# Splitting one routing into pieces on VectorE, and moving the low parts of w2 to GpSimd in whole tiles

## The chip, the cores and the metric

One Trainium2 chip, one of its cores. The metric is the device time of one launch in microseconds (us). TensorE (PE) does the matrix products, VectorE (DVE), ScalarE (ACT) and GpSimd (POOL) the elementwise work; SyncE (SP) and GpSimd issue the DMA transfers.

## What is computed

An mLSTM attention over 2 x 8 heads, 768 steps, head width 40; its output, as 1536 tokens of width 320, goes through a dense layer with softplus (320 to 2048 to 320), and the result through a mixture of 8 experts, in which each token takes the one expert with the largest logit. The part of the reference that the change lies in:

```python
def _moe2_ref(x, w_gate, w_output_gate, w1, w2):
    logits = x @ w_gate
    e_idx = np.argmax(logits, axis=1)
    ...                       # gate_w: the chosen expert's softmax weight; eom: a sigmoid gate
    for e in range(E):
        mask = e_idx == e
        h = np.maximum(x[mask] @ w1[e], 0.0)
        ye = h @ w2[e]
        out[mask] = gate_w[mask, None] * eom[mask, e, None] * ye
```

Everything is float32. The kernel forms the large products from operands split into a rounded high part and a low part (the rest), so that three products of the faster type (high x high, high x low, low x high) stand for one float32 product.

## The kernel before

**A planner orders the work.** The kernel is written as Python generators, the tasks. Each `yield "V"` (or "A", "G", "P", "S") is a request for a turn on VectorE (ScalarE, GpSimd, TensorE, SyncE); "VG" or "AV" leaves the planner the choice between two; `yield [events]` waits. `Weaver.run` (line 118) keeps a clock for each engine, made up of fixed costs, and gives the next turn to the task that can start first by these clocks, ties by rank. All instructions that a task issues between two yields go into the engine's queue in one piece. On the chip each engine then works through its queue in just that order and waits where an operand is not there, whether or not something behind it could run. A change of the yields so changes the order in the queues, and the planner's costs decide how.

**Dense layer and routing.** The 1536 tokens are cut into 6 blocks of 256 (`NBLK`, blk = 0 to 5). `up1` (line 1255) makes the products `ph` of a block with one of 16 column groups f, in PSUM banks of the ring `bank_h`; `softplus` (1227) does three ScalarE activations on `ab` (two buffers), then on VectorE `g` (which frees the `ab` buffer and the PSUM bank of `ph`), then the cast `gh` and the difference `gl`; `down1` (1278) adds the products of `gh` and `gl` with the second weight into `acc`. When a block's sum is near its end, `down1` starts `route(blk)` (915). It computes logits, counts tokens per expert with small products, and gives each token a row number (`posi`) in a table `rows` in DRAM that is sorted by expert in slots of 128 rows. Two `scatter` tasks (1207, indirect DMAs on GpSimd's queue) write the block's rows. The tail of `route` also carries the state (room left, next free slot) to the next block's routing, `state[blk + 1]`. This tail is 28 small VectorE instructions. Between its steps stands `yield from pause(blk)`, and `pause` (1051) yields in all blocks but blk = `NBLK - 2` = 4, the next to last. So the tail of block 4 is one piece in VectorE's queue, while the others can be interleaved with `g` and `gl`. Block 5 has a tail of its own, `place_last`.

**What waits for the scatters of block 4.** `early_rows` (1123) loads the first four slots (`er`) from `rows` once ten scatters, those of blocks 0 to 4, are done; `early_turn` (1152) transposes them on TensorE (`xe`) and adds the tokens of block 5 from the chip's own memory, so that the experts can begin before block 5 is in DRAM.

**Experts.** There are 15 slots (`NS`), each of one expert. The hidden width 1024 is done in 4 quarters of 256 columns (`NQ`, qn = 0 to 3). In each quarter `second` (1638) does, for pairs of slots, `up` (products `ph` with `w1s`, three PSUM banks), `halves_sum` (1581: a ScalarE copy `hr` and a VectorE sum `hr`), `turn_h` (1590: transposes `tp` into two PSUM banks) and `split_h` (1600: ScalarE `hh`, VectorE `hl`, which frees the bank of `tp`); then for all slots `down` (products `yp` with `w2s`) and `reduce2` (adds into `yac`). In the last quarter, `down` of the first slots is mixed in after slot 9, and each finished slot is written out by an indirect DMA from GpSimd.

**Weights.** For each quarter and expert, `w1raw` and `w2raw` come from DRAM into one ring of 7 buffers. `split_w2` (1422) casts the high part of a tile (128 x 640) on ScalarE, once the last `yp` of the quarter before has read the old `w2s`; `low_w2` (1448) subtracts it from the raw tile, which gives the low part, in two halves of 128 x 320: quarter 0 on GpSimd, the others "VG", on whichever of VectorE and GpSimd is free first by the planner's clocks. `w2_ready[qn]` needs all 8 experts before the first `yp` of the quarter. The raw buffer is free when both halves are done, and the next load in SyncE's queue waits for it: the load of expert 7 takes the buffer of expert 0. `low_w1` and `low_w1p` (1410, 1416) do the same for `w1`, at the end of a quarter.

Of the kernel before, what the change touches and what calls it, by code (L numbers as in the profile page):

```python
# [8 lines left out]
F32 = mybir.dt.float32  # L9
# [225 lines left out]
def mlstm_moe_kernel(ctx: ExitStack, tc: tile.TileContext, q_t, k_t, k, v, i_gate, f_gate, o_gate,  # L235
                     w_in, w_gate, w_og, w1, w2, out):
    nc = tc.nc
    W = Weaver()
# [8 lines left out]
    NQ, E, FQ = w1.shape[0], w1.shape[1], w1.shape[-1]  # L247
# [6 lines left out]
    NBLK = NCH  # L254
# [10 lines left out]
    G = B * H  # L265
# [524 lines left out]
    def psub(out_, a, b_):  # L790
        POOL.tensor_tensor(out=out_, in0=a, in1=b_, op=ALU.subtract)

    def vsub(out_, a, b_):
        DVE.tensor_tensor(out=out_, in0=a, in1=b_, op=ALU.subtract)
# [77 lines left out]
    def tt(out_, a, b_, op):  # L872
        DVE.tensor_tensor(out=out_, in0=a, in1=b_, op=op)
# [4 lines left out]
    def over(ap, n):  # L878
        return ap.unsqueeze(1).to_broadcast([ap.shape[0], n, ap.shape[1]])
# [35 lines left out]
    def route(blk, acc, full, part):  # L915
# [88 lines left out]
        yield "V"  # L1004
        tt(an, tot, room, ALU.is_gt)
        DVE.scalar_tensor_tensor(out=bn, in0=room, scalar=float(P), in1=tot, op0=ALU.add, op1=ALU.is_lt)
        yield from pause(blk)
        DVE.tensor_tensor_scan(out=cum, data0=newp, data1=more_p, initial=0.0, op0=ALU.add, op1=ALU.add)
        tt(m, rank, over(room, T2), ALU.is_ge)
        tt(nr, rank, over(nxt, T2), ALU.add)  # L1010
        yield from pause(blk)
        DVE.scalar_tensor_tensor(out=dn, in0=u, scalar=float(P), in1=base, op0=ALU.mult, op1=ALU.subtract)
        yield from pause(blk)
        tt(m, m, over(dn, T2), ALU.mult)
        DVE.tensor_scalar(out=ef, in0=ef, scalar1=1.0, scalar2=None, op0=ALU.add)
        yield from pause(blk)
        tt(nr, nr, m, ALU.add)
        DVE.scalar_tensor_tensor(out=ef, in0=ssum, scalar=1e-9, in1=ef, op0=ALU.add, op1=ALU.mult)
        yield from pause(blk)
        tt(nr, nr, ohb, ALU.mult)  # L1020
        DVE.reciprocal(out=row[:, :, CCOL], in_=ef)
        yield from pause(blk)
        DVE.tensor_reduce(out=pos, in_=nr, axis=AX.X, op=ALU.add)
        yield from pause(blk)
        DVE.tensor_copy(out=posi, in_=pos)
        placed = Event(W.cur.out)
        for t in range(T2):
            W.add(after(placed, after(whole[t], scatter(blk * TPB + t, row[:, t, :], posi[:, t:t + 1], row_ev))), 0)
        yield from pause(blk)
        tt(t8, an, dn, ALU.mult)  # L1030
        tt(c1, csi, rem.to_broadcast([P, E]), ALU.is_le)
        tt(room, room, tot, ALU.subtract)
        tt(c2, an, bn, ALU.add)
        yield from pause(blk)
        tt(nxt, nxt, t8, ALU.add)
        DVE.tensor_reduce(out=nmx[:, 0:1], in_=c1, axis=AX.X, op=ALU.add)
        tt(nmx[:, 1:2], total, rem, ALU.is_gt)
        DVE.scalar_tensor_tensor(out=room, in0=c2, scalar=float(P), in1=room, op0=ALU.mult, op1=ALU.add)
        DVE.scalar_tensor_tensor(out=s128, in0=total, scalar=float(P), in1=s128, op0=ALU.mult, op1=ALU.add)
        yield from pause(blk)  # L1040
        tt(nxt, nxt, tot, ALU.add)
        DVE.scalar_tensor_tensor(out=nmx[:, 1:2], in0=rem, scalar=0.0, in1=nmx[:, 1:2], op0=ALU.is_ge, op1=ALU.mult)
        W.signal(ev)
        yield from pause(blk)
        DVE.scalar_tensor_tensor(out=base, in0=room, scalar=s128, in1=nxt, op0=ALU.subtract, op1=ALU.add)
        DVE.scalar_tensor_tensor(out=esl, in0=nmx[:, 0:1], scalar=nmx[:, 1:2], in1=esl, op0=ALU.mult, op1=ALU.add)
        tt(rem, rem, total, ALU.subtract)
        W.signal(small_ev)
        W.signal(state[blk + 1])

    def pause(blk):
        if blk != NBLK - 2:
            yield "V"

    def place_last(small, tot, rank, ohb, ef, ssum, row, row_ev, ev, counts_ev, small_ev, blk, whole):
        T2, T8 = TPB, TPB * E
# [150 lines left out]
    def scatter(i, row, posi, row_ev):  # L1207
        yield "G"
        r = POOL.indirect_dma_start(
            out=rows, out_offset=bass.IndirectOffsetOnAxis(ap=posi, axis=0), in_=row, in_offset=None,  # L1210
            bounds_check=SLOTS * P - 1, oob_is_err=True)
        if i:
            tc.declare_no_dep(r.ins, group="scatter", reason="every token has a row of its own")
        tc.add_to_no_dep_group("scatter", r.ins)
        W.signal(row_ev)
        W.signal(scattered)
        if i < NTILE - TPB:
            W.signal(scattered_most)
# [55 lines left out]
    def after(t, gen):  # L1274
        yield [t if isinstance(t, Event) else Event(t)]
        yield from gen

    def down1():
        parts = {}
        yield [done_chunk[b][0] for b in range(B)]  # L1280
        for blk, f0, f1 in legs:
            acc, full = [], events(TPB)
            for t in range(TPB):
                acc.append((yield from bank_y.get([P, DM], F32, f"acc{t}")))
            if f1 < NF:
                if f0 == 0:
                    parts[blk] = (yield from row_ring.get([P, TPB, ROW], F32, "row", users=TPB)) + (None,)
                before, parts[blk] = parts[blk][2], parts[blk][0:2] + (events(TPB),)
            for f in range(f0, f1):
                yield [done_g[blk, f]]  # L1290
                gh, gl, e1, e2 = g_t.pop((blk, f))
                for t in range(TPB):
                    yield "P"
                    sl = slice(t * P, (t + 1) * P)
                    PE.matmul(acc[t][0], gh[:, sl], w_down(f, 0), start=f == f0, stop=False)
                    PE.matmul(acc[t][0], gh[:, sl], w_down(f, 1), start=False, stop=False)
                    PE.matmul(acc[t][0], gl[:, sl], w_down(f, 0), start=False, stop=f == f1 - 1)
                    if f == f1 - 1:
                        if f1 < NF:
                            W.add(after(W.cur.out, keep_part(*acc[t], parts[blk], t, before)), 1)  # L1300
                        else:
                            W.signal(full[t])
                W.signal(e1)
                W.signal(e2)
                W.signal(used_w[f])
                if f == NF - 2:
                    W.add(route(blk, acc, full, parts.get(blk)), 1)
# [14 lines left out]
    right = {}  # L1322
# [99 lines left out]
    def split_w2(qn):  # L1422
        if qn:
            yield [w2_read[qn - 1]]
        else:
            yield [down_done]
            right["w2s"] = big.tile([P, 2, 2, E, DM], F32R, tag="win", name="w2s")
        w2s = right["w2s"]
        for e in range(E):
            yield [w2_raw[qn, e]] + ([have_exps if e < E - 2 else begun[e - 4]] if qn == 0 else [])  # L1430
            r, ev = w2_t.pop((qn, e))
            yield "AV" if qn else "A"
            copy(w2s[:, 0, :, e, :], r)
            W.add(after(W.cur.out if qn else clear, low_w2(qn, e, r, ev)), 3.9)
# [11 lines left out]
        W.signal(clear)  # L1446

    def low_w2(qn, e, r, ev):
        for j in range(2):
            yield "VG" if qn else "G"  # L1450
            (psub if W.cur.on == "G" else vsub)(right["w2s"][:, 1, j, e], r[:, j], right["w2s"][:, 0, j, e].bitcast(F32))
        W.signal(ev)
        W.signal(w2_ready[qn])

# [71 lines left out]
    rp, w1s, w2s = right["pool"], right["w1s"], right["w2s"]  # L1526
# [291 lines left out]
```

## Time and profile before

| what | us |
|---|---|
| three runs: median (lowest to highest) | 429.84 (429.53 to 431.52) |
| the profiled execution: its own time | 428.57 |
| its span from first to last instruction | 426.9 |
| TensorE busy | 408.9 |
| VectorE busy | 341.4 |
| ScalarE busy | 302.1 |
| GpSimd busy | 186.0 |

The profile is one execution. Its granted TensorE clock was 0.996 of full speed over the span. The busy times say which engine has most to do on the whole; what a stage is worth has to be read in that stage, from the order of the instructions and from what each of them waited for.

### The profile page before, as it was taken

The numbers are of one execution on the slowest core, as the hardware profiler recorded it, in microseconds if no ns is written. First come the engines' busy times: TensorE is split into PE (matmuls) and PEld (weight loads), VectorE is DVE, ScalarE is ACT, GpSimd is POOL, SyncE is SP. The second block draws the span as 40 slices with busy tenths as digits, with TensorE's granted clock in tenths as the row PEclk, the third lists the DMA queues.
The fourth block names the chain that finished last, engine by engine and source line by source line (L and its number), as shares of the span: only waits on it lengthen the run. The fifth ranks groups of instructions, "written<-read, shape, count | busy, mean of one in ns | idle before, by whom it ended". The sixth has DMA issues, their size and how long they took to land.

```text
span 426.9 us, 9922 instructions
## 1 busy us (share of the span) xinstructions
PE 408.9 (96%) x3095; PEld 388.6 (91%) x3095; DVE 341.4 (80%) x914; ACT 302.1 (71%) x880; POOL 186.0 (44%) x272
## 2 busy tenths in 40 slices
PE   8899999999999999999999999989999999999994
PEld 7787999999989999999999999767998998898893
DVE  4998979889988999997765765767755898898863
ACT  3678889969767877876967887576798666565421
POOL 5265755665041102130210101237676487387665
PEclk9999999999999999999999999999999999999998
DMA  8959595571228981222100101318645745645022
GB/s 264 339 176 335 188 306 188 180 223 36 87 60 281 340 272 55 64 63 62 39 36 4 39 2 40 111 38 271 227 136 173 237 136 194 215 130 157 13 83 96
DMA packets 32284, 62.90 MB, mean 147 GB/s; under 512 B 4218, under 2 KB 16765, under 8 KB 32230
## 3 DMA queue, kind: packets, MB, share of 16 engines
q1 hardware_dynamic: 30742, 57.87, 43.1%
q0 software_dynamic: 1488, 4.35, 2.8%
q8 instruction: 28, 0.46, 0.5%
q14 instruction: 26, 0.21, 0.2%
HBM read 54.05 MB, written 8.65 MB: 147 GB/s over the span
## 4 chain that ended last, share of the span: by engine, by line
PE 71%; DMA 9%; DVE 7%; issue 4%; ACT 4%; POOL 3%; SPq 1%; POOLq 0%; ACTq 0%; DVEq 0%
PE ph L196 26%; PE acc L196 19%; PE yp L196 9%; PE pv L196 3%; PE sp L196 3%; DMA out_dram<-yac,tki 2%; PE tp L196 2%; DMA abc<-abc_dram 2%; DMA wra<-in_w_in_dram 2%; PE lg L196 2%; DMA vn<-in_v_dram 2%; POOL w2s L196 1%; DMA yac<-rows 1%; POOL out_dram L196 1%; SPq L196 1%
## 5 line engine op out<-in xcount | busy, mean ns | idle before, releaser
L196 ACT ACTIVATE ab<-ab 128x256 f32<-128x256 f32 x192 | 77.3, 415 | 2.6
L196 PE MATMUL ph<-w1s,flat 128*128 x312 | 60.7, 332 | 0.5 <-ACT flat L196 0.5
L196 POOL TENSOR_TENSOR w1s<-w1raw,w1s 64x256 fp32r<-64x256 f32 (+1 forms) x39 | 40.9, 1061 | 42.5 <-ACT w1s L196 22.0
L196 PE MATMUL acc<-win,gh 128*128 128x320 f32 x240 | 55.7, 317 | 0.0
L196 PE MATMUL yp<-w2s,hh 128*128 x240 | 54.6, 315 | 0.0
L196 DVE SCALAR_TENSOR_TENSOR g<-ph,ab 128x256 f32<-128x256 f32 x96 | 39.8, 419 | 15.9 <-ACT ab L196 15.0
L196 PEld LDWEIGHTS ph<-w1s,flat 128*128 128x128 f32 x312 | 46.7, 189 | 4.7 <-ACT flat L196 0.7
L196 ACT ACTIVATE ab<-ph 128x256 f32<-128x256 f32 x96 | 36.3, 378 | 17.5 <-PE ph L196 16.7
L196 DVE TENSOR_TENSOR gl<-g,gh 128x256 fp32r<-128x256 f32 x96 | 42.2, 445 | 7.7 <-ACT gh L196 6.7
L196 POOL TENSOR_TENSOR w2s<-w2raw,w2s 128x320 fp32r<-128x320 f32 x46 | 42.2, 952 | 8.9 <-ACT w2s L196 3.6
L196 POOL DMA_INDIRECT rows<-row,rsm x12 | 13.1, 1090 | 75.7 <-DVE nxt L196 29.7
L196 ACT CAST gh<-g 128x256 fp32r<-128x256 f32 x94 | 37.3, 398 | 11.1 <-DVE g L196 10.6
L196 ACT COPY hr<-ph 128x256 f32<-128x256 f32 x60 | 22.7, 378 | 29.5 <-PE ph L196 27.9
L196 PE MATMUL ph<-win 128*128 128x256 f32 x250 | 41.3, 286 | 0.6 <-DVE g L196 0.6
L196 PEld LDWEIGHTS yp<-w2s,hh 128*128 128x128 f32 x240 | 39.8, 188 | 1.5 <-issue 0.6
L196 DVE TENSOR_TENSOR hr<-ph,hr 128x256 f32<-128x256 f32 x60 | 24.7, 418 | 18.6 <-ACT hr L196 18.0
L196 PEld LDWEIGHTS acc<-win,gh 128*128 128x128 f32 x240 | 38.7, 189 | 0.5 <-ACT gh L196 0.2
L196 PE MATMUL acc<-win,gl 128*128 128x320 f32 x120 | 37.3, 311 | 0.0
L196 PE MATMUL yp<-w2s,hl 128*128 x120 | 37.2, 310 | 0.0
L196 PEld LDWEIGHTS ph<-win 128*128 128x128 f32 x250 | 34.4, 190 | 0.8 <-DVE g L196 0.8
L196 PE MATMUL acc<-wou,gh 128*128 128x320 f32 x144 | 33.3, 316 | 0.0
L196 ACT CAST w2s<-w2raw 128x640 fp32r<-128x640 f32 x32 | 22.8, 741 | 14.0 <-PE yp L196 14.0
(211 smaller groups left out, 1073.8 us busy)
## 6 DMA issues: line engine op xcount, KB each, us to landing
w1raw<-in_w_dram SPq DMA_DIRECT2D x32, 384.0 KB, 3.1
wra<-in_w_in_dram SPq DMA_DIRECT2D x16, 704.0 KB, 6.6
w2raw<-in_w_dram SPq DMA_DIRECT2D x32, 320.0 KB, 3.5
abc<-abc_dram SPq DMA_DIRECT2D x4, 1024.0 KB
rows<-pad SPq DMA_DIRECT2D x19, 194.0 KB, 6.0
qT<-in_q_t_dram SPq DMA_DIRECT2D x6, 512.0 KB, 4.6
kn<-in_k_dram SPq DMA_DIRECT2D x5, 416.0 KB, 7.5
vn<-in_v_dram SPq DMA_DIRECT2D x6, 320.0 KB, 5.7
```

Of the source, the lines that this page charges most:

```text
L196: return fn(*args, **kw)
```

## The change

Two edits. `pause` loses its argument and yields in every block, so the tail of the routing of block 4 is cut into twelve pieces, as in blocks 0 to 3. And `low_w2` makes the low part of a tile in one GpSimd instruction of 128 x 640 in quarters 0 to 2 and, in quarter 3, for six of the eight experts; experts 3 and 7 of quarter 3 are done in two halves on VectorE.

```diff
-        yield from pause(blk)
+        yield from pause()
         DVE.tensor_tensor_scan(out=cum, data0=newp, data1=more_p, initial=0.0, op0=ALU.add, op1=ALU.add)
...
-    def pause(blk):
-        if blk != NBLK - 2:
-            yield "V"
+    def pause():
+        yield "V"
...
     def low_w2(qn, e, r, ev):
-        for j in range(2):
-            yield "VG" if qn else "G"
-            (psub if W.cur.on == "G" else vsub)(right["w2s"][:, 1, j, e], r[:, j], right["w2s"][:, 0, j, e].bitcast(F32))
+        if qn < NQ - 1 or e % 4 != 3:
+            yield "G"
+            psub(right["w2s"][:, 1, :, e, :], r, right["w2s"][:, 0, :, e, :].bitcast(F32))
+        else:
+            for j in range(2):
+                yield "V"
+                vsub(right["w2s"][:, 1, j, e], r[:, j], right["w2s"][:, 0, j, e].bitcast(F32))
         W.signal(ev)
         W.signal(w2_ready[qn])
```

The first pair of lines stands for all eleven calls of `pause` in `route`, which change alike.

## Rows read from the trace of the kernel before

**Rows 1.** The page: shares of the span by engine in the chain that ended last.
```profile
PE 71%; DMA 9%; DVE 7%; issue 4%; ACT 4%; POOL 3%; SPq 1%; POOLq 0%; ACTq 0%; DVEq 0%
```
**Rows 2.** Timeline, routing of block 4 (start, us, engine, out<-in, count [idle before <-releaser]).
```profile
267.05 0.41 ACT L196 ACTIVATE ab<-ab 128x256 f32<-128x256 f32 x1
267.10 0.17 DVE L196 TENSOR_TENSOR newp<-lg,room 128x8 f32<-128x8 f32 x1 [0.86 <-ACT rsm L196]
268.65 0.17 DVE L196 CAST rsm<-rsm 128x2 uint32<-128x2 f32 x1
270.00 0.74 DVE L196 SCALAR_TENSOR_TENSOR g<-ph,ab 128x256 f32<-128x256 f32 x2
270.44 0.41 ACT L196 CAST gh<-g 128x256 fp32r<-128x256 f32 x1 [1.38 <-DVE g L196]
270.46 0.74 PE L196 MATMUL ph<-xh,wou 128*128 128x256 f32 x4 [0.81 <-DVE g L196]
```
**Rows 3.** Timeline: second scatter of block 4, load of the early rows, their first use.
```profile
270.98 1.17 POOL L196 DMA_INDIRECT rows<-row,rsm  x1 [0.30 <-ACT gh L196]
273.83 0.89 SPq L196 DMA_DIRECT2D er<-rows  x2
279.99 0.31 PE L196 MATMUL xe<-ident,er 128*128 128x128 f32 x1
```
**Rows 4.** Timeline of VectorE, routing of block 3: first step and row numbers.
```profile
251.46 0.17 DVE L196 TENSOR_TENSOR newp<-lg,room 128x8 f32<-128x8 f32 x1
254.38 0.16 DVE L196 CAST rsm<-rsm 128x2 uint32<-128x2 f32 x1
```
**Rows 5.** Waits from 300 us on (total us, times, longest us).
```profile
PE tp L196 <- DVE hl L196: 2.1, 3, 1.0
```
**Rows 6.** Timeline, start of quarter 2.
```profile
356.99 9.63 POOL L196 TENSOR_TENSOR w2s<-w2raw,w2s 128x320 fp32r<-128x320 f32 x10 [2.51 <-DVE yac L196]
358.15 0.33 SPq L196 DMA_DIRECT2D w2raw<-in_w_dram  x1
360.39 1.92 DVE L196 TENSOR_TENSOR w2s<-w2raw,w2s 128x320 fp32r<-128x320 f32 x2
360.95 0.69 ACT L196 ACTIVATE hh<-tp 128x256 fp32r<-128x256 f32 x2
362.57 0.74 DVE L196 SCALAR_TENSOR_TENSOR hl<-tp,hh 128x256 fp32r<-128x256 f32 x2
362.63 0.79 ACT L196 CAST w2s<-w2raw 128x640 fp32r<-128x640 f32 x1
363.03 0.77 PE L196 MATMUL tp<-ident,hr 128*128 128x128 f32 x4 [0.99 <-DVE hl L196]
```
**Rows 7.** Timeline, quarters 1 and 3: low parts on GpSimd, TensorE's wait, first product.
```profile
325.46 3.89 POOL L196 TENSOR_TENSOR w2s<-w2raw,w2s 128x320 fp32r<-128x320 f32 x4 [3.41 <-ACT w2s L196]
389.66 9.62 POOL L196 TENSOR_TENSOR w2s<-w2raw,w2s 128x320 fp32r<-128x320 f32 x10 [2.60 <-issue]
395.70 0.77 PE L196 MATMUL tp<-ident,hr 128*128 128x128 f32 x4 [0.89 <-DVE hl L196]
400.95 0.54 PE L196 MATMUL yp<-w2s,hh 128*128 x2
```
**Rows 8.** Chain that ended last (start, us, what): first products with w2 in quarters 1 and 2.
```profile
341.51 1.75 PE yp L196 x12
374.10 1.75 PE yp L196 x12
```
**Rows 9.** By tile and by line: low parts; durations (ns min/median/max), or busy us, mean ns.
```profile
L196 POOL TENSOR_TENSOR w2s<-w2raw,w2s x46: 858/882/1145, 287.0 to 398.4; 128x320 fp32r<-128x320 f32 x46
L196 DVE TENSOR_TENSOR w2s<-w2raw,w2s x18: 492/1054/1202, 326.3 to 398.6; 128x320 fp32r<-128x320 f32 x18
L196 POOL TENSOR_TENSOR w1s<-w1raw,w1s 128x512 fp32r<-128x512 f32 x1 | 1.3, 1283 | 7.6 <-ACT w1s L196 7.6
L196 POOL TENSOR_TENSOR w1s<-w1raw,w1s 128x512 fp32r<-128x512 f32 x1 | 1.6, 1618 | 0.1
```

More of the change, by code (lines that the diff above doesn't have):

```diff
@@ L1010, in route @@
         tt(nr, rank, over(nxt, T2), ALU.add)
-        yield from pause(blk)
+        yield from pause()
         DVE.scalar_tensor_tensor(out=dn, in0=u, scalar=float(P), in1=base, op0=ALU.mult, op1=ALU.subtract)
-        yield from pause(blk)
+        yield from pause()
         tt(m, m, over(dn, T2), ALU.mult)
         DVE.tensor_scalar(out=ef, in0=ef, scalar1=1.0, scalar2=None, op0=ALU.add)
-        yield from pause(blk)
+        yield from pause()
         tt(nr, nr, m, ALU.add)
         DVE.scalar_tensor_tensor(out=ef, in0=ssum, scalar=1e-9, in1=ef, op0=ALU.add, op1=ALU.mult)
-        yield from pause(blk)
+        yield from pause()
         tt(nr, nr, ohb, ALU.mult)
         DVE.reciprocal(out=row[:, :, CCOL], in_=ef)
-        yield from pause(blk)
+        yield from pause()
         DVE.tensor_reduce(out=pos, in_=nr, axis=AX.X, op=ALU.add)
-        yield from pause(blk)
+        yield from pause()
         DVE.tensor_copy(out=posi, in_=pos)
@@ L1028, in route @@
             W.add(after(placed, after(whole[t], scatter(blk * TPB + t, row[:, t, :], posi[:, t:t + 1], row_ev))), 0)
-        yield from pause(blk)
+        yield from pause()
         tt(t8, an, dn, ALU.mult)
@@ L1033, in route @@
         tt(c2, an, bn, ALU.add)
-        yield from pause(blk)
+        yield from pause()
         tt(nxt, nxt, t8, ALU.add)
@@ L1039, in route @@
         DVE.scalar_tensor_tensor(out=s128, in0=total, scalar=float(P), in1=s128, op0=ALU.mult, op1=ALU.add)
-        yield from pause(blk)
+        yield from pause()
         tt(nxt, nxt, tot, ALU.add)
@@ L1043, in route @@
         W.signal(ev)
-        yield from pause(blk)
+        yield from pause()
         DVE.scalar_tensor_tensor(out=base, in0=room, scalar=s128, in1=nxt, op0=ALU.subtract, op1=ALU.add)
```

## The prediction

> **What bounds the kernel now.** I read the chain that ended last first: 71% of its time is TensorE's, no other engine has more than 9% [rows 1]. So the end is set by TensorE's queue, and what the change is worth is the sum of the gaps in that queue that it closes, less those that it opens. I then read the timeline at the places that the two edits touch, looking for an idle time ahead of a TensorE instruction and for who ended it.
>
> Place A is the routing of block 4. Its tail begins on VectorE at 267.10 and holds the engine without a break until 270.00, when `g` comes [rows 2]. This `g` is f = 11 of block 5, and its input was ready long before: the last ScalarE step on `ab` began at 267.05 and took 0.41, so it ended at 267.46 [rows 2]. Behind it two others stood: ScalarE was idle for 1.38 us until `gh`, and TensorE for 0.81 us until `ph` could have a PSUM bank back; both waits were ended by `g` [rows 2].
>
> Place B is the start of quarters 1 to 3. From 300 us on, TensorE waits for `hl` three times, 2.1 us in total [rows 5]: 0.99 in quarter 2 [rows 6], 0.89 in quarter 3 [rows 7], so 0.2 is left for quarter 1. In quarter 2 one sees why: `hh` was finished at 361.64, but VectorE was in two halves of low parts from 360.39 to 362.31, and `hl` came at 362.57 [rows 6].
>
> **Edit 1, the routing in pieces.** It removes and adds no instruction; it changes VectorE's order. With a yield after each step, `g` can go in front of most of the tail, at about 267.5 to 268, instead of 270.00. The gain on TensorE is at least the bubble it ends, 0.81 us, and at most the 1.38 by which ScalarE's chain for the last column groups could start earlier [rows 2]; I take 1.0. What is late next is TensorE itself, which has the products `acc` queued.
>
> What moves back is the tail itself, with both scatters on GpSimd's queue and, behind them, the load of the early rows on SyncE's. In block 3, whose tail is in pieces, the row numbers came 2.92 us after the first step (251.46 to 254.38) [rows 4]; in block 4's one piece 1.55 us (267.10 to 268.65) [rows 2]. So they come 0 to 1.4 us later: nothing if the few `g` and `gl` then ready go behind, 1.4 as in block 3. Now the second scatter starts at 270.98, the load is issued at 273.83 in two transfers, 0.89 us for both, and TensorE first needs it at 279.99 [rows 3]. From issue to first use there are 6.2 us. After the change 6.2 - 1.4 - 1.0 = 3.8 would be left in the worst case. A load of weights took 4.5 us at most to land (estimate, from `w2raw`: the issue at 358.15, the cast of that tile at 362.63 [rows 6]). So the load stays hidden, or costs up to 4.5 - 3.8 = 0.7; I take 0, since either delay is at its worst in that. If that cover is gone, the transposes `xe` wait and, behind them in TensorE's queue, the token counts of block 5, which are on the path. The state for block 5's routing is needed more than 10 us later and costs nothing.
>
> **Edit 2, low parts on GpSimd.** Of the 18 halves on VectorE [rows 9] four remain, in quarter 3. No 128 x 640 on GpSimd is in the trace. A 128 x 320 took 858 ns at the least, a 128 x 512 took 1283 [rows 9]: 425 ns for 192 more columns, 2.2 ns each; a whole tile is then 1283 + 128 x 2.2 = 1.57 us. The bounds: two halves at 858 give 1.72, at their largest, 1145, 2.29; the largest 128 x 512, 1618, scaled by 640/512 gives 2.02. I take 1.57, the nearest clean row, since in quarters 1 and 2 no VectorE subtraction runs beside it any more.
>
> Quarter 1: from 325.46 [rows 7], 8 x 1.57 = 12.6, to 338.0; the first `yp` is at 341.51 [rows 8]. Quarter 2: from 356.99 [rows 6] to 369.5, needed at 374.10 [rows 8] less what is gained there. So GpSimd's longer work is hidden, with some 3 us to spare. Quarter 3: from 389.66 [rows 7], 6 x 1.57 = 9.4, plus four VectorE halves beside it. Ten halves in quarter 2 took 9.63 us [rows 6] instead of 10 x 0.858, 1.05 more with six VectorE halves beside them, 0.17 each; four make 0.7. That ends at 399.8; the first `yp` is at 400.95 [rows 7]. Hidden, with about 1 us to spare. In quarter 0 GpSimd does the same work in fewer instructions, long before its first `yp`: nothing.
>
> With the halves gone from VectorE, quarter 1 gains its 0.2. Quarter 2: `hl` can come right after `hh`, at about 361.5, and TensorE finds it when the products before are through: 0.99 at most. Against that stands the raw buffer. The load of expert 7 was issued at 358.15, when expert 0 was done, and its cast on ScalarE began at 362.63 [rows 6]. Expert 0 as a whole ends at 356.99 + 1.57 = 358.56, 0.4 later, so the cast may be 0.4 late, and `hh` of the next slots is queued behind it. I take 0.8 (0.6 to 1.0).
>
> Quarter 3 keeps four halves. First the rows: a half took 492 ns alone and 1054 in the middle, 1202 at most, beside GpSimd's halves of 858 [rows 9]; it waits up to 0.71 us for an instruction that lasts 0.86. The Trainium skill, "SBUF — State Buffer", section "Who interferes with whom", says that a VectorE instruction with two SBUF inputs and a GpSimd instruction that reads SBUF shut each other out for a whole instruction. The trace agrees, as far as 492 against 1202 ns shows it; by that rule the waits grow with GpSimd's longer tiles, and the sum would be that of the third rival, without it the one below. By rows alone: if the wait scales with the instruction in front, 0.71 x 1.57/0.858 = 1.3 us, a half takes up to 1.8. The halves of expert 3 fall just where `hl` is late now. Two of them, 2 x 1.8 = 3.6 at worst and 2 x 1.05 = 2.1 in the middle, stand where by the pattern of quarter 2 three stood, one of 1.05 and a pair of 1.92 [rows 6, 9], 3.0. So quarter 3 lies between a gain of 0.9 (the whole wait goes) and a loss of 0.6, which I put at 0.9 in case expert 7's halves hold `hl` once more. I take a gain of 0.3.
>
> **Sum.** 1.0 + 0.2 + 0.8 + 0.3 = 2.3 us. The profiled execution took 428.57, 1.67 more than its span of 426.9, and would take 426.3. The median of the runs is 1.27 above the profiled execution, so I forecast 429.84 - 2.3 = 427.5. About 0.5%, 2.15 us, is what a measurement of this kernel can tell from no change: faster means below 427.69, slower above 431.99.
>
> **Rivals.** *More than forecast.* All waits go and place A gives nearly its upper end: 1.3 + 0.2 + 1.0 + 0.9 = 3.4, 426.4. For it: VectorE has few other things to do at each place. Against it: the halves left in quarter 3. Chance 0.15.
>
> *Edit 1 does not do what it says.* The planner may still put the twelve pieces one behind the other, if by its clocks `g` is ready late; then A gives 0 and the time is 428.5. Against it: in block 3 the way to the row numbers took nearly twice as long (2.92 against 1.55), so the pieces were interleaved [rows 2, 4]. Chance 0.13.
>
> *Longer waits for GpSimd in quarter 3.* The remaining halves wait behind whole tiles as worked out above; quarter 3 loses 0.9 in place of the 0.3 gained, and the time is 428.7. It decides once a half takes more than 1.5 us. For it: the spread of 492 to 1202 ns [rows 9]. Chance 0.12.
>
> *Slower: GpSimd becomes the bound.* The first `yp` of a quarter needs all eight low parts. GpSimd decides from (341.3 - 325.46)/8 = 1.98 us a tile in quarter 1, (373.3 - 356.99)/8 = 2.04 in quarter 2, and (400.7 - 389.66)/6 = 1.84 in quarter 3. At 2.29, the bound from the slowest half, it ends at 343.8, 375.3 and 403.4, after 341.51, 374.10 and 400.95: 2.3 + 1.2 + 2.4 = 5.9 late against before, less the 1.0 of A, so 4.9 slower, 434.7. For it: one 128 x 512 took 1618 ns [rows 9]. Against it: that one had a VectorE subtraction beside it, and in quarters 1 and 2 these are gone. Chance 0.08.
>
> **How the numbers follow.** The forecast has 0.52, of which about 0.34 lies below 427.69. With the 0.15 of the first rival, faster gets 0.49; the rest of the forecast, 0.18, and the second and third rivals make 0.43 for no change; slower 0.08. The range must hold the first three rivals and the bounds around the forecast: the gain may be 3.9 (3.4, and with new orders elsewhere 0.5 more) or nothing but A's lower end with quarter 3 at its worst and the early rows late (0.81 + 0.2 + 0.6 - 0.9 - 0.7 = 0). So 425.9 to 429.8.
>
> **What would show it.** A: `g` of f = 11 before 268.5, no wait ahead of the last `ph`, the same `xe` without a wait for the load. B: no wait of `tp` for `hl` in quarters 1 and 2; tiles of 1.5 to 1.7 us on GpSimd; the first `yp` not waiting for GpSimd. In quarter 3, the duration of the four VectorE halves, and whether `tp` still waits. The prediction is wrong if whole tiles take over 1.9 us, if the tail stays in one block, or if the planner, whose clocks change from 267 us on, puts other work ahead of `hr` and `hl`.

## The result, and the profile after

The changed kernel took 425.70 us (median; 424.02 to 426.28, seven runs), the kernel before 429.53 in the same series (428.16 to 431.52, seven runs). The ratio is 0.9906, with a 95% interval of 0.9882 to 0.993: 3.8 us less, between 3.0 and 5.1. The forecast was 427.5 with a range of 425.9 to 429.8. The direction was right, the gain was over half as large again as forecast, and the time lies 0.2 below the range. Of the 1.8 between forecast and time, 0.3 is the median of the kernel before, 429.53 here and 429.84 in the three runs that the forecast started from. Two executions below, one of edit 1 alone (450.73) and one of GpSimd in halves (448.84), had a mean granted clock of 0.85 and are left out of the medians.

The chain that ended last, by engine (page of the changed kernel), beside [rows 1]:

```profile
PE 87%; DVE 5%; ACT 3%; DMA 2%; POOL 1%; issue 1%; SPq 1%; POOLq 0%; ACTq 0%
```

TensorE's share of the chain went from 71% to 87%. That is not the gain: 16 points of a span of 424 us are 68 us, and the time fell by 3.8. The chain is followed back from the last instruction, and it goes through other instructions now, also where neither edit changes anything: the load of `abc` at 49.31 us, 8.70 us long, was on the chain before and is not now. With GpSimd in halves, a kernel below that is faster than the one before too, the share is 76%. What the change is worth has to be read stage by stage.

The routing of block 4 in the changed kernel, from its timeline (start, us, engine, out<-in, count, idle before), beside [rows 2, 3]:

```profile
266.77 0.17 DVE L196 TENSOR_TENSOR newp<-lg,room 128x8 f32<-128x8 f32 x1 [0.86 <-ACT rsm L196]
267.17 0.43 DVE L196 SCALAR_TENSOR_TENSOR g<-ph,ab 128x256 f32<-128x256 f32 x1 [0.16 <-ACT ab L196]
268.17 0.42 DVE L196 TENSOR_TENSOR gl<-g,gh 128x256 fp32r<-128x256 f32 x1 [0.26 <-ACT gh L196]
269.17 0.45 PE L196 MATMUL acc<-win,gh 128*128 128x320 f32 x2
269.61 0.45 PE L196 MATMUL acc<-win,gh 128*128 128x320 f32 x2
270.05 0.75 PE L196 MATMUL ph<-xh,wou 128*128 128x256 f32 x5
270.23 0.16 DVE L196 CAST rsm<-rsm 128x2 uint32<-128x2 f32 x1
272.55 0.97 POOL L196 DMA_INDIRECT rows<-row,rsm  x1 [0.30 <-ACT ab L196]
275.19 0.89 SPq L196 DMA_DIRECT2D er<-rows  x2
279.71 0.17 PE L196 MATMUL counts<-rsm,tri 128*128 128x8 bf16 x1 [0.66 <-DVE rsm L196]
279.84 2.24 PE L196 MATMUL xe<-ident,er 128*128 128x128 f32 x12
```

`g` of f = 11 comes 0.40 us after the tail's first step instead of 2.90, its `gl` follows at 268.17 inside the tail, and the last `ph` waits for nothing. The row numbers come 3.46 us after the first step (266.77 to 270.23) instead of 1.55, so 1.9 later. The early rows are then loaded 4.65 us ahead of their first use, and `xe` does not wait for them. The order on TensorE differs in two places. Two groups of `acc` products (269.17 and 269.61) now stand ahead of the last `ph`; before, all of them stood behind it. And the counts of block 5 now stand ahead of all twelve early transposes, where four stood ahead of them, with 0.66 us of idle time in front, where it was 0.18.

The start of quarter 2 and the first product of quarter 3 in the changed kernel, same view, beside [rows 6, 7], and its first `yp` of quarters 1 and 2 on the chain, beside [rows 8]:

```profile
356.20 12.26 POOL L196 TENSOR_TENSOR w2s<-w2raw,w2s 128x640 fp32r<-128x640 f32 x8 [2.43 <-issue]
357.79 0.33 SPq L196 DMA_DIRECT2D w2raw<-in_w_dram  x1
360.04 0.75 DVE L196 SCALAR_TENSOR_TENSOR hl<-tp,hh 128x256 fp32r<-128x256 f32 x2
361.19 0.60 PE L196 MATMUL tp<-ident,hr 128*128 128x128 f32 x4
362.39 0.80 ACT L196 CAST w2s<-w2raw 128x640 fp32r<-128x640 f32 x1
397.92 0.54 PE L196 MATMUL yp<-w2s,hh 128*128 x2
```

```profile
340.81 1.75 PE yp L196 x12
372.01 1.75 PE yp L196 x12
```

`hl` now ends at 360.79, ahead of the transposes at 361.19, and no row of waits "PE tp <- DVE hl" as in [rows 5] is left from 300 us on. GpSimd is done at 368.46, 3.4 us before the first `yp` (371.84; the chain's row begins 0.17 later, and those of [rows 8] 0.16).

The low parts by tile in the changed kernel (ns min/median/max), beside [rows 9]:

```profile
L196 POOL TENSOR_TENSOR w2s<-w2raw,w2s x30: 1548/1566/1836, 285.5 to 395.7; 128x640 fp32r<-128x640 f32 x30
L196 DVE TENSOR_TENSOR w2s<-w2raw,w2s x4: 478/840/1525, 389.9 to 397.7; 128x320 fp32r<-128x320 f32 x4
```

**Where the time went, stage by stage.** Whole times of single executions of one kernel spread over 1 to 5 us. The way from one fixed instruction to another inside an execution spreads far less in most stages, so I cut every profiled execution at the same six instructions: the counts of block 0 at about 201 us (one expectation below calls them those of block 1), VectorE's first step of `S` (about 283), the first `yp` of each quarter and the last `yp`. The entries are differences of start times in us. The last four kernels ran on another chip, where the kernel before took 432.75; of the 4.3 by which the changed kernel's profiled execution is longer there, 0.9 stand in the last column and 3.0 behind the last `yp`.

| kernel | counts to `S` | to quarter 0 | to quarter 1 | to quarter 2 | to quarter 3 | to last `yp` |
|---|---|---|---|---|---|---|
| before | 82.67 | 26.31 | 31.64 | 32.59 | 27.01 | 19.36 |
| changed | 81.50 | 27.78 | 31.00 | 31.19 | 26.08 | 19.36 |
| changed, again | 81.50 | 25.82 | 30.99 | 31.21 | 26.07 | 19.36 |
| edit 1 alone | 81.50 | 27.28 | 31.60 | 32.63 | 27.03 | 19.36 |
| edit 2 alone | 82.68 | 26.64 | 30.98 | 31.22 | 26.05 | 19.36 |
| one break | 82.30 | 26.94 | 30.98 | 31.24 | 26.08 | 19.37 |
| quarter 3 all on GpSimd | 81.51 | 26.01 | 30.97 | 31.21 | 25.75 | 21.49 |
| GpSimd in halves | 81.50 | 27.78 | 31.00 | 31.35 | 25.76 | 20.00 |
| five warming products | 81.46 | 26.06 | 30.99 | 31.20 | 26.07 | 19.36 |
| five and seven | 81.50 | 26.72 | 30.98 | 31.23 | 26.09 | 19.36 |
| experts 1 and 5 (other chip) | 81.48 | 25.90 | 30.98 | 31.20 | 27.07 | 20.31 |
| experts 0 and 4 (other chip) | 81.51 | 26.61 | 30.99 | 31.21 | 25.72 | 20.54 |
| changed (other chip) | 81.48 | 26.54 | 30.97 | 31.18 | 26.06 | 20.30 |
| five warming products (other chip) | 81.50 | 26.33 | 30.99 | 31.20 | 26.06 | 20.69 |

The change is worth 1.17 in the first column, 0.64, 1.40 and 0.93 in quarters 1 to 3: 4.14 us. The second column differs from execution to execution, from 25.8 to 27.8, also for one and the same kernel; the forecast had no term for it. With it, the two profiled executions of the change took 2.7 and 4.6 less than the one before from the counts to the last `yp`.

### The profile page after: what moved, and what is told of

Its sections match the earlier page's. It is cut to its first block, busy times and chain, and to the rows that moved or that the text cites. A ratio compares the mean times of both kernels' runs of the same rounds, so it can differ in the third digit from the quotient of the medians.

```text
span 423.9 us, 9886 instructions
## 1 busy us (share of the span) xinstructions
PE 409.6 (97%) x3095; PEld 390.7 (92%) x3095; DVE 330.6 (78%) x900; ACT 301.2 (71%) x880; POOL 189.6 (45%) x256
## 4 chain that ended last, share of the span: by engine, by line
PE 87%; DVE 5%; ACT 3%; DMA 2%; POOL 1%; issue 1%; SPq 1%; POOLq 0%; ACTq 0%
PE ph L196 34%; PE acc L196 20%; PE yp L196 13%; PE pv L196 5%; PE sp L196 4%; PE tp L196 3%; PE lg L196 2%; DMA wra<-in_w_in_dram 2%; PE qc L196 2%; PE xe L196 1%; PE kv L196 1%; PE x2tp L196 1%; DVE wta L196 1%; PE xp L196 1%; SPq L196 1%
## 5 line engine op out<-in xcount | busy, mean ns | idle before, releaser
L196 POOL TENSOR_TENSOR w2s<-w2raw,w2s 128x640 fp32r<-128x640 f32 x30 | 46.9, 1593 | 8.5 <-issue 5.0
```

What stands on the lines that cost most here:

```text
L196: return fn(*args, **kw)
```

## The experiments

**The two edits alone.** First the changed kernel again, on the same chip as the next ones, where the kernel before took 429.45 (25 runs).

> The changed kernel again, on the same chip as the single edits. Theory 1 (what the traces of before and after show): edit 2 is worth about 2.7 us and edit 1 about 1.2, of which nothing is left in executions in which the granted clock falls to 0.5 to 0.7 of full speed around 281 to 287 us; so 2.7 to 3.9 us less than before, and two groups of runs, about 1.2 us apart. Theory 2 (the terms of the forecast): 2.3 less, whatever the clock does.

Measured: 425.50 (423.63 to 426.4, 6 runs), ratio 0.9896 (0.9861 to 0.993). That is 4.0 less, just past the upper end of theory 1 and not the 2.3 of theory 2 (the interval gives 3.0 to 6.0); two groups of runs are not to be seen. In the profiled execution the clock stayed at 1.00.

Edit 1 alone:

```diff
     def pause(blk):
-        if blk != NBLK - 2:
-            yield "V"
+        yield "V"
```

> Edit 1 alone: the routing of block 4 in pieces, low parts of w2 as before. Theory 1: 1.2 us less than before where the clock stays up behind the idle time ahead of the counts of block 5, nothing where it falls; median 0 to 1.2 less. Theory 2 (forecast): 1.0 less. Theory 3 (the gain of edit 1 is always hidden, because the loads of rows set the end of that stage): 0 in every execution, whatever the clock, with the first yp of quarter 0 at 309.8 as before.

Measured: 428.47 (eleven runs), ratio 0.9977 (0.9955 to 0.9999): 1.0 less by the medians, between 0.0 and 1.9, which theories 1 and 2 fit alike. The first stage is shorter by the same 1.17 as in the changed kernel, the quarters are as before. In this execution the granted clock fell after the counts, and `xslot` waited 0.92 for rows from DRAM (0.5 in the kernel before); the second stage took 1.0 more, and of the 1.17 only 0.2 was left at the first `yp`. Theory 3 says that this is always so, and the table speaks against it. From the counts to the first `yp` of quarter 0, its first two columns together, the kernel before takes 109.0 and edit 2 alone 109.3; the seven executions with all breaks and the clock at 1.00 take 107.3 to 108.2, the four with all breaks and the clock at 0.50 take 108.1 to 109.3. So the gain of edit 1 reached the first `yp` in every execution in which the clock stayed up, and was lost in part or as a whole in those in which it fell.

Edit 2 alone (cut at the dots; all of the change in `low_w2`):

```diff
-        for j in range(2):
-            yield "VG" if qn else "G"
...
+        if qn < NQ - 1 or e % 4 != 3:
+            yield "G"
+            psub(right["w2s"][:, 1, :, e, :], r, right["w2s"][:, 0, :, e, :].bitcast(F32))
...
```

> Edit 2 alone: low parts of w2 as in the change, the routing of block 4 in one piece as before. Theory 1: about 2.7 us less than before (0.6 in quarter 1, 1.4 in quarter 2, 0.7 in quarter 3), because each wait for hl also stretched the transposes behind it. Theory 2 (forecast): 0.2 + 0.8 + 0.3 = 1.3 less. Theory 3: with edit 1 worth nothing, all of the 3.8.

Measured: 427.36, ratio 0.9944 (0.9918 to 0.9969), so 2.1 us by the medians and at most 3.5, less than the 3.8 of theory 3. The stages are clearer: 0.66, 1.37 and 0.96 in quarters 1 to 3, 3.0 in all, against the forecast's 1.3. Theory 1 had the first two; in quarter 3 it was 0.25 too low, because it took the chain's grouped `yp` row as the start.

Why a wait costs more than its idle time is seen by laying the two side by side in quarter 2. TensorE's timeline, edit 1 alone (low parts as before):

```profile
360.83 2.12 PE L196 MATMUL ph<-w1s,flat 128*128 x12
363.95 0.77 PE L196 MATMUL tp<-ident,hr 128*128 128x128 f32 x4 [1.00 <-DVE hl L196]
364.47 2.12 PE L196 MATMUL ph<-w1s,flat 128*128 x12
366.43 0.69 PE L196 MATMUL tp<-ident,hr 128*128 128x128 f32 x4
366.88 2.13 PE L196 MATMUL ph<-w1s,flat 128*128 x12
```

Edit 2 alone:

```profile
360.84 2.13 PE L196 MATMUL ph<-w1s,flat 128*128 x12
362.81 0.60 PE L196 MATMUL tp<-ident,hr 128*128 128x128 f32 x4
363.16 2.12 PE L196 MATMUL ph<-w1s,flat 128*128 x12
365.12 0.60 PE L196 MATMUL tp<-ident,hr 128*128 128x128 f32 x4
```

Without a wait, one pair of slots takes 2.32 us from `ph` to `ph` (360.84 to 363.16). With the wait it takes 3.64 (360.83 to 364.47), 1.32 more, of which the view calls only 1.00 idle. The transposes normally begin 0.16 ahead of the recorded end of the products before them (362.81 against 362.97); that overlap is lost. And `hl` frees the two banks one after the other, so four transposes take 0.77 in place of 0.60. The pair behind takes 2.41, another 0.09. That makes 1.00 + 0.16 + 0.17 + 0.09 = 1.42; the stages say 1.41 (32.63 against 31.22). The ends of products are modelled in the profile; the starts, on which the 2.32 and 3.64 rest, are not affected by that.

**One break in the tail.** The changed kernel, with a single yield in block 4, after the tail's first step, instead of eleven. The other ten calls stay `pause(blk)`, as in the kernel before, against which the edit is shown (the line of `bn` is cut).

```diff
         DVE.scalar_tensor_tensor(out=bn, in0=room, ...)
-        yield from pause(blk)
+        yield "V"
         DVE.tensor_tensor_scan(out=cum, ...)
```

> The changed kernel with a single break in the tail of block 4's routing, after its first step, instead of eleven. Theory 1 (edit 1 pays because g gets in front of the tail): g of f = 11 comes at about 267.5 as with all breaks, the way from the counts of block 1 to the logits of block 5 is shorter by the same 1.17 us, and the row numbers come no more than 0.8 us later than in one piece (1.55 us after the first step, plus one g of 0.37 or a pair of 0.74), not 1.9. Rival (the later steps must be interleaved too, since gl and the next g are held up as well): less than 0.8 of the 1.17.

Measured: 426.66, ratio 0.9949 (0.9923 to 0.9975); the first stage gains only 0.37 of the 1.17. The rival was right, though `g` came 0.40 after the first step, as with all breaks, and the row numbers only 0.45 later than in one piece, as theory 1 says. This and the next two kernels ran where the kernel before took 428.91 (26 runs) and the changed kernel has no run, so they are compared by ratio and by stage. Timelines of VectorE and TensorE, one break:

```profile
268.19 0.43 DVE L196 SCALAR_TENSOR_TENSOR g<-ph,ab 128x256 f32<-128x256 f32 x1 [0.16 <-ACT ab L196]
270.19 0.76 PE L196 MATMUL ph<-xh,wou 128*128 128x256 f32 x5
271.14 0.41 DVE L196 TENSOR_TENSOR gl<-g,gh 128x256 fp32r<-128x256 f32 x1
```

```profile
273.98 0.46 PE L196 MATMUL acc<-win,gh 128*128 128x320 f32 x2
274.27 0.31 PE L196 MATMUL acc<-win,gl 128*128 128x320 f32 x1
274.71 0.56 PE L196 MATMUL acc<-win,gh 128*128 128x320 f32 x2
275.40 0.42 PE L196 MATMUL acc<-win,gl 128*128 128x320 f32 x1
275.66 0.47 PE L196 MATMUL acc<-win,gh 128*128 128x320 f32 x2
```

`g` is in front and the wait of `ph` is gone, but its `gl` stands behind the tail: 2.95 us after `g`, against 1.00 in the changed kernel. The products `acc`, in groups of three that follow each other by 0.44 us when nothing waits, then come late (273.98 to 274.71 to 275.66, so 0.73 and 0.95). TensorE in the kernel before, for comparison:

```profile
269.14 0.52 PE L196 MATMUL ph<-xl,win 128*128 128x256 f32 x3
270.46 0.86 PE L196 MATMUL ph<-xh,wou 128*128 128x256 f32 x5 [0.81 <-DVE g L196]
271.16 0.52 PE L196 MATMUL ph<-xl,wou 128*128 128x256 f32 x3
```

Here the last `ph` starts 1.32 after the three products ahead of it, where 0.36 is usual, and its first five take 0.70 from start to start in place of 0.60: the wait cost 1.06, not 0.81. The groups of `acc` behind it lose, beyond 0.44 each, 0.76 in the kernel before, 0.64 in the changed kernel and 1.45 with one break. So one break wins 1.06 and gives 0.69 of it back, which leaves the 0.37; all breaks win 1.06 and 0.12. The bubble of [rows 2] was one of two things that the tail held up, and the other showed once the first was gone.

**Quarter 3 wholly on GpSimd.**

```diff
-        if qn < NQ - 1 or e % 4 != 3:
+        if True:
```

> The changed kernel, but in the last quarter too all eight whole tiles on GpSimd, none on VectorE. Theory 1 (GpSimd is then the bound of quarter 3): eight tiles of 1.57 us from 387.6 end at 400.2, 2.0 us after the 398.2 at which the first yp starts in the changed kernel; from the first yp of quarter 2 to the first of quarter 3 28.2 instead of 26.2, the time 2.0 more. Rival (what is left of waiting in quarter 3 comes from the VectorE halves, which wait for GpSimd): without them 0.4 to 1.0 us less.

Measured: 427.13, ratio 0.9936 (0.9911 to 0.9961); from quarter 2 to the last `yp` 47.24 in place of 45.44, so 1.8 slower. Timeline, quarter 3:

```profile
387.56 12.21 POOL L196 TENSOR_TENSOR w2s<-w2raw,w2s 128x640 fp32r<-128x640 f32 x8 [2.59 <-issue]
399.82 0.41 PE L196 MATMUL yp<-w2s,hh 128*128 x1 [1.86 <-POOL w2s L196]
```

Theory 1 holds, though not where it looked: TensorE's first product of quarter 3 is not late, but GpSimd ends at 399.77 and the second product waits 1.86 for it. But the rival's mechanism is there too, since the way to the first `yp` falls from 26.08 to 25.75. So 0.33 is what the VectorE halves still cost in quarter 3, and 1.8 is what they save on the whole.

**GpSimd in halves.** The placement of the change, the old size (the removed lines are cut at the dots).

```diff
-        if qn < NQ - 1 or e % 4 != 3:
-            yield "G"
-            psub(right["w2s"][:, 1, :, e, :], r, right["w2s"][:, 0, :, e, :].bitcast(F32))
...
+        on_v = qn == NQ - 1 and e % 4 == 3
+        for j in range(2):
+            yield "V" if on_v else "G"
+            (vsub if on_v else psub)(right["w2s"][:, 1, j, e], r[:, j], right["w2s"][:, 0, j, e].bitcast(F32))
```

> The changed kernel with the same engines for the low parts, but each of GpSimd's tiles in two halves of 128 x 320, as before. Theory 1 (what counts is that the halves leave VectorE; the whole tile only saves GpSimd time that is hidden): quarters 1 and 2 as in the changed kernel (31.0 and 31.2 us from first yp to first yp), GpSimd at 16 x 0.86 = 13.8 us; quarter 3 at 12 x 0.86 + 0.7 = 11.0 from 387.6 ends at 398.6, 0 to 0.5 later than now. If the waits of VectorE's halves scale with the GpSimd instruction in front, the longest of the four falls from 1.5 to 1.2 us or less. Rival: the whole tiles are part of the gain; then quarters 1 and 2 lose some of their 0.6 and 1.4.

Measured: 427.17 (eleven runs), ratio 0.9945 (0.9924 to 0.9966); the profiled execution had a lowered clock in the second stage. By stages quarter 1 is the same, quarter 2 0.15 longer, and from quarter 2 to the last `yp` 45.76 in place of 45.44. Low parts by tile in quarter 3, GpSimd in halves:

```profile
L196 POOL TENSOR_TENSOR w2s<-w2raw,w2s x12: 872/886/1142, 388.8 to 399.0; 128x320 fp32r<-128x320 f32 x12
L196 DVE TENSOR_TENSOR w2s<-w2raw,w2s x4: 580/621/827, 391.1 to 397.7; 128x320 fp32r<-128x320 f32 x4
```

So nearly all of edit 2's gain is the placement; the whole tile saves the last 0.5, 0.15 in quarter 2 and 0.3 in quarter 3, where GpSimd is nearly the bound. VectorE's longest half fell from 1525 to 827 ns, as the theory of scaling waits asks; but in the kernel before a half took up to 1202 beside the same short tiles [rows 9], so the length of the instruction in front is not all that sets the wait.

**Other experts on VectorE.** `e % 4 != 1` and `e % 4 != 0` in place of `e % 4 != 3`.

> The changed kernel with experts 1 and 5, not 3 and 7, in halves on VectorE in the last quarter. Theory (the 26.1 us from the first yp of quarter 2 to the first of quarter 3 still hold 0.3 of waiting, because the half of expert 3 at 394.6 waits behind a whole tile on GpSimd for 1.0 us just ahead of an hr; 25.76 is what is left without it): the halves of expert 1 fall earlier, 25.8 to 26.1, and GpSimd's last tile ends at 397.6 as now. Rival: they fall on other hr and hl, and the stretch is 26.1 or longer.

Measured: 429.70 in one execution, quarter 3 at 27.07, the rival. Waits in the timeline, experts 1 and 5:

```profile
388.91 1.21 PE L196 MATMUL ph<-w1s,flat 128*128 x6 [0.41 <-DVE hr L196]
392.79 0.77 PE L196 MATMUL tp<-ident,hr 128*128 128x128 f32 x4 [0.35 <-DVE hl L196]
```

The halves stand in front of one `hr` and one `hl`, and all of quarter 3's gain is lost: which two experts stay on VectorE is worth 1 us here, in one execution of each.

> The same with experts 0 and 4 on VectorE. Theory: as with experts 1 and 5, 25.8 to 26.1, with GpSimd starting one cast later (0.7 us), so its last tile may end at 398.3 and hold up the first yp by some 0.3. Rival: 26.1 or longer.

Measured: 429.52 in one execution, quarter 3 at 25.72, so the last 0.33 goes, but GpSimd starts a cast later and the weight load of TensorE's second `yp` waits 0.28 for it; from quarter 2 to the last `yp` 46.26 against 46.36 of the changed kernel on that chip. That is 0.1, less than these runs can tell apart.

**The clock.** In the changed kernel's first profiled execution the granted clock fell after the idle time of 0.66 us. Stretches of the span, changed kernel (from:to, length, busy us and count of PE, PEld, DVE, ACT and POOL, then the granted clock, DMA share, GB/s):

```profile
280.00:282.00 2.00, 2.00 (x12) 1.67 (x11) 1.85 (x16) 2.00 (x8) 0.00 (x0) 0.62 0.01 4
282.00:284.00 2.00, 1.58 (x6) 1.43 (x6) 2.00 (x9) 2.00 (x4) 1.19 (x1) 0.50 0.00 0
284.00:286.00 2.00, 2.00 (x9) 1.81 (x9) 0.26 (x2) 0.40 (x1) 1.61 (x4) 0.50 0.33 125
```

The changed kernel again:

```profile
282.00:284.00 2.00, 1.08 (x10) 0.84 (x8) 1.85 (x14) 2.00 (x7) 0.00 (x0) 1.00 0.01 4
```

And what it does to the same twenty products, first the changed kernel, then the changed kernel again:

```profile
282.49 5.32 PE L196 MATMUL xe<-S,part 128*128 128x256 f32 x20 [0.42 <-DVE S L196]
```

```profile
284.23 3.35 PE L196 MATMUL xe<-S,part 128*128 128x256 f32 x20 [1.14 <-DVE S L196]
```

At 0.50, which is 1.2 GHz, for most of that time, they take 5.32 us in place of 3.35. To keep TensorE busy there, the idle time was filled with more warming products.

```diff
-    W.add(warm(have_last_lg, 2), 0)
+    W.add(warm(have_last_lg, 5), 0)
```

> The changed kernel with five extra warming products on TensorE in place of two ahead of the counts of block 5, in the idle time of 0.66 us that stands there (about 0.2 us each; nothing else moves). Theory 1: TensorE is hardly idle there, the granted clock stays at 1.00 from 280 to 288 us in every execution, and the time is that of the changed kernel's better executions, about 1.2 us less than its worse ones; no two groups of runs. Theory 3 (loads of rows set the end of the stage): no change against the changed kernel, or 0.2 us more.

Measured: 425.13, ratio 0.9901 (0.9868 to 0.9933), against 425.50 of the changed kernel: no difference that can be told from the noise. The idle time is gone and the profiled execution stayed at 1.00, but one of the eight executions took 428.82 with a mean clock of 0.991, so what theory 1 says of every execution is not shown.

> The changed kernel with more warming products in both idle times of TensorE near the counts of block 5: five in place of two ahead of the counts, seven in place of three ahead of the use of S (about 0.2 us each). Theory 1 (the clock falls in some executions because of these idle times): no execution with a mean granted clock under 0.994, against 4 of 13 of the changed kernel so far; median 0.3 to 0.6 us under the changed kernel's 425.5. Rival (the clock falls for other reasons): as often as before, and the same median, or up to 0.3 more where the products hold up S.

Measured: 425.68, ratio 0.9919 (0.9889 to 0.995). None of its six executions is under 0.994, as theory 1 says, but six are few, and the time is not lower. The seven stand behind the products with `S` in TensorE's queue, not ahead of them, so the wait for `S` was still 1.15, and the four more of 0.21 us delayed the experts: 26.72 in the second stage, 0.66 more than with five alone.

> The changed kernel once more, beside the next one on the same chip, to count the executions with a lowered mean granted clock. Theory 1 (the idle time of 0.66 us ahead of the counts of block 5 lets the clock fall in some executions): about a third of the executions at 0.994 or less. Rival: no more than the one in five that the kernel before shows.

Measured: 429.27, ratio 0.9919 (0.9896 to 0.9942), on the other chip; four of six executions at 0.994 or less, but there nine of eleven of the kernel before too.

> The changed kernel with five warming products in place of two ahead of the counts of block 5, as before, for the same count. Theory 1: fewer than one in seven executions at 0.994 or less, and a median 0.4 us under the changed kernel's. Rival: as many as in the changed kernel, and the same median.

Measured: 429.32, ratio 0.9921 (0.9897 to 0.9944). No gain, and the count of executions told nothing on this chip. Among the fourteen profiled executions of the table, four had the clock at 0.50 around 283 us (changed, edit 1 alone, GpSimd in halves, experts 0 and 4), all of them with the 0.66 us of idle time; four others with it stayed at 1.00, and so did all six without it. That fits the idle time as a part of the cause and does not show it (where the clock fell in the execution at 0.991 without it is not known). The time that filling it gives is too small to be measured, so no version beats the changed kernel.

## Why the prediction was wrong

**Place A: right in place and nearly in size.** Forecast 1.0 (0.81 to 1.38), measured 1.16 to 1.21 in the profiled executions with all breaks. The reason was incomplete: the wait that I saw was worth 1.06, but with `g` alone in front 0.69 of that is lost again on the products `acc`, and 0.37 is left. The breaks that let `gl` and the next `g` through keep the rest.

**The row numbers: too optimistic.** Forecast 0 to 1.4 later, measured 1.9; block 3 was no upper bound, because here four `g` and `gl` came ahead of them (267.17, 268.17, 269.13 and 269.88), and there three. The cover was as worked out: 4.65 us from issue to first use, no wait of `xe`. That the planner would change TensorE's order too, the counts ahead of the early transposes and two groups of `acc` ahead of the last `ph`, was not in the forecast.

**Place B, quarters 1 to 3: the step that failed.** I took the idle time in front of `tp` as the price of the wait. Forecast 0.2, 0.8 and 0.3; measured 0.64, 1.40 and 0.93. In quarter 2 the prediction even says 0.99 at most. The first two are the idle times of [rows 5 to 7] plus 0.41 to 0.44, and quarter 3, with the 0.33 that the remaining halves cost, is its 0.89 plus 0.37: the lost overlap, the second bank and the pair behind, as laid side by side for quarter 2 above. It was in my rows: `tp` at 0.77 stands in [rows 6], where 0.60 is normal. Place A shows the same: its idle time of 0.81 stood for 1.06. The 0.2 that I took off in quarter 2 for a late raw buffer was not needed: the last cast came 6.19 us after GpSimd's first tile, against 5.64, and nobody waited for it.

**Quarter 3.** The rival of longer waits had the right mechanism and the wrong price. A half took up to 1.525 us, past its point of 1.5, and quarter 3 gained all the same. The Trainium skill, "SBUF — State Buffer", section "Who interferes with whom", has a VectorE instruction with two SBUF inputs contend with a GpSimd instruction that reads SBUF, and calls their shared ports an exclusive lock. The trace agrees as far as a half never waited longer than the tile beside it: beyond the 0.48 of the shortest, 1.05 at most beside tiles of 1.57 us, and 0.35 (0.72 in the kernel before) beside halves of 0.88. But a late half only costs where an `hr` or `hl` stands behind it: 0.33 here, not 1.2, and 1.3 with experts 1 and 5. I priced it as if every half fell so: a cost of 0.6 in the forecast, against 0.33.

**GpSimd: right.** A whole tile was forecast at 1.57 and took 1.566 (median). With 12.3 us for eight tiles, quarters 1 and 2 have 3 us to spare. The rival in which GpSimd sets the end needs one more step than the change takes: with eight tiles in quarter 3 it came true, at 1.8 us.

**The sum and the range.** 1.17 + 0.64 + 1.40 + 0.93 = 4.14 against 2.3, beyond even the rival of more than forecast (3.4). Of the 1.84 between, about 1.2 are the price of the three waits, 0.3 the halves left in quarter 3, 0.2 the raw buffer and 0.2 place A. The medians give 3.8 (3.0 to 5.1); the second column, in which executions of the changed kernel differ by 2.0, is not in the 4.14. The range's lower end was worked out from the same idle times, so it shared their error. The rival in which edit 1 does nothing is out: the pieces were interleaved, and the first stage is 1.17 shorter.

## What to carry to other kernels

Price a wait of the bounding engine by the period of its loop with and without the wait, not by the idle time in the trace: here 1.00 us idle cost 1.41. Before a queue is broken up, list all that stands behind the blocking piece, since the second in line becomes the next wait: one break gave a third of what eleven gave. And where time executions scatter more than the effect, cut the profiled ones at the same instructions: the first stage and quarters 1 to 3 agreed within 0.06 us between executions whose whole times spread over 1 to 5. The stage between them did not (25.8 to 27.8), and there one execution shows little.

## What the runs showed of the hardware that was not expected

TensorE's granted clock fell to 0.50, twice for 3.4 us and twice for 6.8, in four of eight profiled executions of the same instruction order around 283 us, though TensorE had waited no more than 0.66 us in one piece in the 15 us before; the stretch up to the first `yp` then took 26.6 to 27.8 us, against 25.8 to 26.5 in the other four. What decides between the two was not found.
